# Linear attention and a gated convolution layer: queries projected with the tokens moving, their maxima subtracted by a third matmul pass

## The chip, the cores and the metric

One NeuronCore of a Trainium2 chip runs the whole program. The metric is the device time of one execution in microseconds (us), the median of several runs. TensorE (PE) multiplies matrices and writes PSUM; VectorE (DVE), ScalarE (ACT) and GpSimd (POOL) work on elements; SyncE (SP) here only issues DMA transfers, one after the other in a fixed order. Each engine works through its own instructions in order and waits on semaphores for the others.

## The reference

```python
def phi(x):                                   # x: batch 8, heads 8, 576 tokens, 64
    proj = np.einsum('bhsd,df->bhsf', x, w_phi)        # 64 -> 128 features
    proj = proj - np.max(np.abs(proj), axis=-1, keepdims=True)
    return np.concatenate([np.exp(proj), np.exp(-proj)], axis=-1)
q_p, k_p = (phi(q), phi(k))
kv = np.einsum('bhsf,bhsd->bhfd', k_p, v)
z = np.sum(k_p, axis=2)
num = np.einsum('bhsf,bhfd->bhsd', q_p, kv)
den = np.einsum('bhsf,bhf->bhs', q_p, z)[..., None] + 1e-06
attn = num / den                              # then 8 heads side by side: 512 columns
h = np.maximum(x @ w_in, 0.0)                 # 512 -> 1024
# conv_out: three-tap convolution over the tokens, per column
gate = 1.0 / (1.0 + np.exp(-conv_out))
out = h * gate @ w_out                        # 1024 -> 512
```

All inputs and outputs are float32. What matters here is that each token's query projection has the largest absolute value among its 128 features subtracted before the two exponentials.

## The kernel before, in words

**Units and groups.** The attention of a batch is two units (`qd` 0 and 1), each of four heads laid out as two pairs: a query tile has the 64 dimensions of two heads on its 128 partitions and tokens along its columns. A unit is cut into five groups: group 0 has one tile of 128 tokens (the last 64 tokens of both pairs), groups 1 to 4 have two tiles, so a unit has 9 tiles and the 16 units have 144. `k_process` does one group of keys, `q_process` one group of queries.

**Precision.** A float32 operand is cut by `split` into a rounded part `hi` (type fp32r, which TensorE multiplies in one pass) and the rest `lo = x - hi`. A product is then three fp32r passes: hi*hi, hi*lo and lo*hi. An operand that is left as float32 takes two passes, each at half the speed. The first `NQ_F32` = 2 units project their queries in float32.

**A group of queries before.** `load_split` loads a tile `qr` (line 179) and POOL makes `qxh` and `qxl` of it (lines 62 and 65). `project` (lines 199 to 201) multiplies with the tokens as the stationary operand and the block-diagonal weights `wbd` (256 columns: 128 features for each of the two heads) as the moving one, so the result `qp` has tokens on partitions. DVE takes the largest absolute value along the row (`qm`, line 204) and subtracts it (`qs`, line 206). TensorE then turns each 128x128 block (line 320, `tp`), since the next product needs features on partitions. ACT takes both exponentials from PSUM (line 326), `split` makes `qh` and `ql` (ACT line 60, DVE line 65), and the `nm` products (lines 348 and 356) give numerator and denominator. Small transfers carry denominators (line 377, `den`, and line 397, `rr`) to where one operation can divide.

**PSUM.** Pool `pg` has four banks under the tag `g`, shared by key projections, query projections, turned tiles and `nm`. Pool `pm` has two banks for the layer behind the attention, `pk` two for the key-value sums.

**The layer behind.** `h_part` (`hp`, line 429) and `o_part` (`op`, line 488) are long rows of fp32r passes, 24 of them for each of 64 output tiles in `o_part` and 12 for each of 128 in `h_part`; `conv_process` does the convolution and the gate on POOL, DVE and ACT (lines 452 to 475).

**The order.** The program text is not the order of work. A planner at the end of the kernel steps generators: each yields what it costs TensorE (`pe`), how long its inputs take (`wait`, times `LAT` = 1.7), and which named events it needs (`until`). It mixes attention and the layer behind by the work left in each (`ATT_PE`, `MOE_PE`), and up to `WINDOW` attention chains are under way. The order in which instructions are made sets their priority; a scheduler then places each on its engine by priority, as soon as its inputs are ready in the scheduler's own reckoning. `tc.high_priority()` puts instructions ahead of others. The resulting order on each engine is fixed before the kernel runs.

Of the kernel before, what the change touches and what calls it, by code (L numbers as in the profile page):

```python
# [16 lines left out]
F = 128  # L17
DM, FF = 512, 1024
P = 128
# [3 lines left out]
VW = D + 1  # L23
NH = 11

WINDOW = 13
LAT = 1.7
TAIL_US = 24
AHEAD = 300

NQ_F32 = 2
NKV_F32 = 2


# [1 line left out]
def kernel(  # L36
# [41 lines left out]
    split(wbd_f, wbd_hi, wbd_lo, nc.vector, nc.vector)  # L78
    idn = load_const(ident, [P, P], "idn")


    rr = cp.tile([P, S], F32, name="rr")
    nc.gpsimd.memset(rr, 0.0)

# [87 lines left out]
    def load_split(src, b, qd, g, kind):  # L172
        c0, n = group_columns(g)
        if kind == "q" and 2 * b + qd < NQ_F32:
            raw = sb.tile([P, n * P], F32, name=f"{kind}r{b}_{qd}_{g}", tag=kind + "xh", bufs=2)
            nc.sync.dma_start(out=raw, in_=src[b, qd, :, c0 : c0 + n * P])
            return n, raw, None
        raw = sb.tile([P, n * P], F32, name=f"{kind}r{b}_{qd}_{g}", tag=kind + "r", bufs=2)
        nc.sync.dma_start(out=raw, in_=src[b, qd, :, c0 : c0 + n * P])
        hi = sb.tile([P, n * P], F32R, name=f"{kind}xh{b}_{qd}_{g}", tag=kind + "xh", bufs=2)  # L180
        lo = sb.tile([P, n * P], F32R, name=f"{kind}xl{b}_{qd}_{g}", tag=kind + "xl", bufs=2)
        split(raw, hi, lo, nc.gpsimd, nc.gpsimd)
        return n, hi, lo

    def project(n, hi, lo, b, qd, g, kind):

        if b == 0 and kind == "k":

            ps = pm.tile([P, n * 256], F32, name=f"{kind}p{b}_{qd}_{g}", tag="m")
        else:  # L190
            ps = pg.tile([P, n * 256], F32, name=f"{kind}p{b}_{qd}_{g}", tag="g", bufs=4)
        for t in range(n):
            o = ps[:, t * 256 : (t + 1) * 256]
            his = hi[:, t * P : (t + 1) * P]
            if lo is None:
                nc.tensor.matmul(out=o, lhsT=his, rhs=wbd_f, start=True, stop=True)
                continue
            los = lo[:, t * P : (t + 1) * P]
            nc.tensor.matmul(out=o, lhsT=his, rhs=wbd_hi, start=True, stop=False)  # L199
            nc.tensor.matmul(out=o, lhsT=his, rhs=wbd_lo, start=False, stop=False)  # L200
            nc.tensor.matmul(out=o, lhsT=los, rhs=wbd_hi, start=False, stop=True)  # L201
        ps3 = ps.rearrange("p (t f) -> p t f", f=F)
        m = sb.tile([P, 2 * n], F32, name=f"{kind}m{b}_{qd}_{g}", tag="m", bufs=4)
        nc.vector.tensor_reduce(out=m, in_=ps3, axis=AX, op=ALU.max, apply_absolute_value=True)  # L204
        pr = sb.tile([P, 2 * n, F], F32, name=f"{kind}s{b}_{qd}_{g}", tag=kind + "s", bufs=2)
        nc.vector.tensor_tensor(out=pr, in0=ps3, in1=m.unsqueeze(2).broadcast_to([P, 2 * n, F]), op=ALU.subtract)  # L206
        return pr

# [11 lines left out]
    def k_process(b, qd, g):  # L220
        j = (b * NQ + qd) * 5 + g

        def back(key, k):
            return (key, j - k) if j >= k else None

        yield until(back("kp", 2), back("kv", 4))
        n, hi, lo = load_split(kT, b, qd, g, "k")
        v0 = 16 if g == 0 else 4 * (g - 1)
        v = sb.tile([P, 4 * VW], F32, name=f"v{b}_{qd}_{g}", tag="v", bufs=4)
        nc.sync.dma_start(out=v, in_=vt[b, qd, :, v0 * VW : (v0 + 4) * VW])  # L230
        yield wait(3000)
        yield until(back("kv", 2))
        set_ready(("kp", j))
        pr = project(n, hi, lo, b, qd, g, "k")
        e = sb.tile([P, 2, 2 * n, F], F32, name=f"ke{b}_{qd}_{g}", tag="ke", bufs=2)
        nc.scalar.activation(out=e[:, 0], in_=pr, func=AF.Exp)  # L236
        nc.scalar.activation(out=e[:, 1], in_=pr, func=AF.Exp, scale=-1.0)
        yield pe(330 * n)
        yield wait(3000)
        yield until(back("kv", 1))  # L240
        if g == 0:
            kvps[b, qd] = [pk.tile([P, 2, 2 * VW], F32, name=f"kv{b}_{qd}_{i}", tag=f"kv{i}") for i in range(2)]
        kp = kvps[b, qd]

        def products():
            for t in range(n):
                for i in range(2):
                    for s in range(2):
                        lhsT = e[:, s, 2 * t + i, :]
                        if g == 0:  # L250
                            ins = nc.tensor.matmul(out=kp[i][:, s, :], lhsT=lhsT, rhs=v[:, 2 * i * VW : 2 * (i + 1) * VW],  # L251
                                             start=(s == 0), stop=False, skip_group_check=True)
                        else:
# [46 lines left out]
    def q_process(b, qd, g):  # L300
# [7 lines left out]
        yield wait(3000)  # L308
        yield until(back("tp", 2))
        set_ready(("qp", *divmod(j, 5)))  # L310
        pr = project(n, hi, lo, b, qd, g, "q")
        yield pe(330 * n)
        yield wait(1700)
        yield until(back("num", 2))
        set_ready(("tp", *divmod(j, 5)))

        tp = pg.tile([P, 2, n, P], F32, name=f"tp{b}_{qd}_{g}", tag="g", bufs=4)
        for t in range(n):
            for i in range(2):
                nc.tensor.transpose(out=tp[:, i, t, :], in_=pr[:, 2 * t + i, :], identity=idn)  # L320
# [3 lines left out]
        for s in range(2):  # L324
            e = qh[:, s] if f32 else sb.tile([P, 2, n * P], F32, name=f"qe{b}_{qd}_{g}_{s}", tag="qe", bufs=2)
            nc.scalar.activation(out=e, in_=tp.rearrange("p i t s -> p i (t s)"), func=AF.Exp, scale=1.0 - 2.0 * s)  # L326
            if not f32:
                split(e, qh[:, s], ql[:, s], nc.scalar, nc.vector)
        yield pe(220 * n)
# [37 lines left out]
        for pr_, o, s0, w in parts:  # L367
            if (b, qd, pr_) not in den:
                den[b, qd, pr_] = sb.tile([72, 16], F32, name=f"den{b}_{qd}_{pr_}", tag="den", bufs=3)
                numt[b, qd, pr_] = sb.tile([P, S], F32, name=f"num{b}_{qd}_{pr_}", tag="num", bufs=4)  # L370
            dn, nt = den[b, qd, pr_], numt[b, qd, pr_]

            dro = dr[D : D + 1, 2 * o : 2 * (o + w)]
# [149 lines left out]
        active.append([now[0], g, False, lead[0]])  # L523

    MOE_PE = 2 * B * (8 * 1480 + 4 * 2960)
    ATT_PE = B * (18 * 330 + 72 * 215 + 18 * 550 + 8 * 6 * 270 + 4 * 250)
    TAIL = TAIL_US * 1000
    left = {"a": ATT_PE, "m": MOE_PE}
    start = {}
# [113 lines left out]
```

## Time and profile before

| | |
|---|---|
| Median of 3 runs | 825.25 us (824.22 to 826.01) |
| The profiled execution | 825.6 us, span 823.5 us, mean granted TensorE clock 0.989 |
| PE, share of the span busy | 96% |
| PE weight loads (overlap with PE) | 94% |
| DVE | 78% |
| ACT | 69% |
| POOL | 37% |
| DMA queue of SP, share of 16 engines | 20.1% |

The span runs from the first to the last instruction; the 2.1 us between it and the execution's time lie around it. A busy share says how much of the span an engine had an instruction under way. Matmuls overlap one another in the profile: one takes some 0.28 us from start to end, but the next starts much sooner, so the cost of a pass is the distance between the starts of two neighbours, not its duration.

### The profile page before, as it was taken

The page shows a single profiled execution, that of the slowest core. Times are in us where ns is not written, and L with a number is a line of the kernel's source. Part 1 is how long each engine was busy: PE and PEld are TensorE (multiplying, and loading weights), DVE is VectorE, ACT ScalarE, POOL GpSimd, SP SyncE. Part 2 cuts the span into 40 slices and gives each one's busy share as a digit, 9 for nine tenths or more (in the row PEclk, how much of TensorE's full clock was granted, in tenths as well). Part 3 has the DMA queues.
Part 4 walks back from the last instruction along what each step waited for, and adds up shares of the span by engine and source line. Part 5 has one row for each costly group of instructions (what it writes and reads, how often), then busy time and mean ns, then how long its engine had stood idle before and what let it go on. Part 6 is the DMA issues. An engine that isn't in the chain of part 4 may idle for free.

```text
span 823.5 us, 17817 instructions
## 1 busy us (share of the span) xinstructions
PE 788.0 (96%) x6350; PEld 772.5 (94%) x6350; DVE 645.6 (78%) x1390; ACT 569.5 (69%) x1228; POOL 307.6 (37%) x467
## 2 busy tenths in 40 slices
PE   7778779999999999999999999999999999999998
PEld 6767678999999999999999999999999999999998
DVE  4879999799987769787779878788697878766551
ACT  4598777797788867687586857678576867644332
POOL 4757765444443424414233333424334131111110
PEclk9799989999999999999999999999999999999999
DMA  6544421211211302121121211112021100000001
GB/s 187 157 134 135 135 66 47 67 41 44 70 56 44 93 18 71 27 82 50 46 61 43 69 34 60 47 50 82 15 77 29 56 12 19 13 30 30 23 23 44
DMA packets 56328, 49.18 MB, mean 60 GB/s; under 512 B 15024, under 2 KB 54192, under 8 KB 56240
## 3 DMA queue, kind: packets, MB, share of 16 engines
q1 hardware_dynamic: 56240, 48.05, 20.1%
q8 instruction: 51, 0.84, 0.4%
q14 instruction: 37, 0.30, 0.1%
HBM read 38.13 MB, written 9.44 MB: 58 GB/s over the span
## 4 chain that ended last, share of the span: by engine, by line
PE 74%; DVE 10%; ACT 7%; issue 4%; DMA 3%; POOL 1%; SPq 1%; DVEq 0%; ACTq 0%; POOLq 0%
PE op L488 22%; PE hp L429 21%; PE kv L255 8%; PE nm L356 8%; PE tp L320 3%; PE kp L199 2%; PE nm L348 2%; PE kp L200 2%; PE kp L201 2%; PE qp L199 1%; PE qp L200 1%; PE qp L201 1%; DMA w_r<-in_w_in_dram 1%; PE kv L251 1%; DVE qm L204 1%
## 5 line engine op out<-in xcount | busy, mean ns | idle before, releaser
L457 DVE SCALAR_TENSOR_TENSOR c<-h,cw,c 128x287 f32<-128x287 f32 (+1 forms) x256 | 138.7, 554 | 49.4 <-POOL c L452 47.5
L452 POOL TENSOR_SCALAR c<-h,cw 128x288 f32<-128x288 f32 x128 | 75.0, 588 | 243.6 <-ACT h L436 184.3
L255 PE MATMUL kv<-v,ke 128*128 128x65 f32 x1024 | 159.4, 255 | 1.4 <-ACT ke L236 1.2
L255 PEld LDWEIGHTS kv<-v,ke 128*128 128x128 f32 x1024 | 153.5, 193 | 4.8 <-ACT ke L236 1.8
L429 PE MATMUL hp<-xh,win_hi 128*128 128x290 f32 x512 | 153.2, 300 | 0.6 <-ACT os L493 0.6
L429 PE MATMUL hp<-xl,win_hi 128*128 128x290 f32 x512 | 152.7, 298 | 0.2 <-DVE xl L65 0.2
L488 PE MATMUL op<-gh,wout_hi 128*128 128x288 f32 x512 | 152.2, 298 | 0.0
L429 PE MATMUL hp<-xh,win_lo 128*128 128x290 f32 x512 | 151.9, 297 | 0.0
L488 PE MATMUL op<-gl,wout_hi 128*128 128x288 f32 x512 | 151.4, 296 | 0.0
L488 PE MATMUL op<-gh,wout_lo 128*128 128x288 f32 x512 | 150.9, 295 | 0.0
L436 ACT ACTIVATE h<-hp 128x290 f32<-128x290 f32 x128 | 52.2, 414 | 71.7 <-PE hp L429 71.2
L429 PEld LDWEIGHTS hp<-xh,win_hi 128*128 128x128 f32 x512 | 96.7, 190 | 1.5 <-ACT os L493 1.4
L62 POOL TENSOR_SCALAR kxh<-kr 128x256 fp32r<-128x256 f32 (+1 forms) x80 | 43.8, 547 | 144.1 <-PE kp L200 134.6
L429 PEld LDWEIGHTS hp<-xl,win_hi 128*128 128x128 f32 x512 | 97.0, 189 | 0.6 <-DVE xl L65 0.6
L429 PEld LDWEIGHTS hp<-xh,win_lo 128*128 128x128 f32 x512 | 97.1, 190 | 0.0
L488 PEld LDWEIGHTS op<-gh,wout_lo 128*128 128x128 f32 x512 | 96.4, 188 | 0.0
L488 PEld LDWEIGHTS op<-gl,wout_hi 128*128 128x128 f32 x512 | 96.2, 188 | 0.0
L488 PEld LDWEIGHTS op<-gh,wout_hi 128*128 128x128 f32 x512 | 96.1, 188 | 0.0
L65 DVE TENSOR_TENSOR ql<-qe,qh 128x512 fp32r<-128x512 f32 x112 | 79.9, 732 | 9.9 <-ACT qh L60 9.5
L236 ACT ACTIVATE ke<-ks 128x512 f32<-128x512 f32 (+1 forms) x80 | 46.9, 586 | 39.1 <-DVE ks L206 36.5
L326 ACT ACTIVATE qe<-tp 128x512 f32<-128x512 f32 x112 | 61.2, 595 | 12.2 <-PE tp L320 10.4
L356 PE MATMUL nm<-ql,kvh 128*65 128x256 f32 x224 | 68.4, 308 | 0.3 <-DVE ql L65 0.2
(84 smaller groups left out, 1989.5 us busy)
## 6 DMA issues: line engine op xcount, KB each, us to landing
v<-in_vt_dram SPq DMA_DIRECT2D x80, 130.0 KB
out_dram<-os SPq DMA_DIRECT2D x64, 144.0 KB
qr<-in_qT_dram SPq DMA_DIRECT2D x64, 128.0 KB
kr<-in_kT_dram SPq DMA_DIRECT2D x64, 128.0 KB
w_r<-in_w_in_dram SPq DMA_DIRECT2D x8, 512.0 KB
w_r<-in_w_out_dram SPq DMA_DIRECT2D x8, 512.0 KB
rr<-rc SPq DMA_DIRECT2D x128, 2.2 KB
qr<-in_qT_dram SPq DMA_DIRECT2D x16, 64.0 KB
```

Source lines behind the costliest of these rows:

```text
L62: nc.gpsimd.tensor_scalar(out=hi, in0=src, scalar1=1.0, scalar2=0.0, op0=ALU.mult, op1=ALU.add)
L65: eng_lo.tensor_tensor(out=lo, in0=src, in1=hi.bitcast(F32), op=ALU.subtract)
L199: nc.tensor.matmul(out=o, lhsT=his, rhs=wbd_hi, start=True, stop=False)
L236: nc.scalar.activation(out=e[:, 0], in_=pr, func=AF.Exp)
L255: ins = nc.tensor.matmul(out=kp[i][:, s, p0 : p0 + VW], lhsT=lhsT, rhs=v[:, (2 * t + i) * VW : (2 * t + i + 1) * VW], start=False, stop=(g ...
L326: nc.scalar.activation(out=e, in_=tp.rearrange("p i t s -> p i (t s)"), func=AF.Exp, scale=1.0 - 2.0 * s)
L356: ins = after(ins, lambda: nc.tensor.matmul(out=ps[:, i, o : o + w], lhsT=w_, rhs=x_, start=(k == 0), stop=(k == 5)))
L429: nc.tensor.matmul(out=ps, lhsT=w_, rhs=x_, start=(k == 0), stop=(k == 11))
L436: nc.scalar.activation(out=hs, in_=ps, func=AF.Relu)
L452: nc.gpsimd.tensor_scalar(out=cv, in0=hs[:, o : o + TC], scalar1=cw[:, f, 1:2], scalar2=0.0, op0=ALU.mult, op1=ALU.add)
L457: nc.vector.scalar_tensor_tensor(out=cv[:, lo:hi], in0=hs[:, o + j - 1 + lo : o + j - 1 + hi], scalar=cw[:, f, j : j + 1], in1=cv[:, lo:hi ...
L488: nc.tensor.matmul(out=ps, lhsT=w_, rhs=x_, start=(k == 0), stop=(k == 23))
```

## The change

From unit 4 on (`NQ_F32` = 4, so from the third batch) a group of queries goes another way; units 2 and 3 move from three fp32r passes to float32.

The input tile `qx` now has 128 partitions for one head at a time: rows 0 to 63 hold the rounded query, rows 64 to 127 the rest; the two heads and the tiles of the group lie side by side in up to 512 columns. To that end the query is loaded twice (two DMAs), ACT rounds all 128 rows and POOL subtracts on the lower 64. The weights are stationary: `wq_hi` holds the rounded weights in both halves, `wq_lo` the rest of the weights over rows 0 to 63 and zeros below. Two passes of up to 512 columns give the whole projection with features on partitions, so nothing has to be turned. The maximum now runs across partitions: DVE takes it inside blocks of 32 features with a transposing reduction (`qmt`, 16 columns of 128 rows), three ACT copies bring the four blocks of partitions together, three small DVE operations form the maximum as a rounded part and a rest (in `mx`), a DVE transpose lays them out as rows (`qmp`), and two DMAs write them over rows 64 and 65 of `qx`. A third pass with `wq_m`, which is -1 in those two rows and 0 elsewhere, adds minus the maximum to the PSUM bank. Both exponentials then read this bank as before.

Buffers: `WINDOW` 13 to 16; `qs` 3 instead of 2 for queries, `v` and `num` 3 instead of 4. The planner's costs for TensorE follow.

```diff
-WINDOW = 13
+WINDOW = 16
-NQ_F32 = 2
+NQ_F32 = 4
...
+    for i in range(2):
+        r = slice(D * i, D * i + D)
+        nc.gpsimd.tensor_copy(out=wq_hi[r, :], in_=wbd_hi[r, i * F : (i + 1) * F].bitcast(F32))
+    nc.gpsimd.tensor_copy(out=wq_m, in_=rr[:, 0:F])
+    nc.gpsimd.tensor_copy(out=wq_lo, in_=rr[:, 0:F])
+    nc.gpsimd.tensor_copy(out=wq_lo[0:D, :], in_=wbd_lo[0:D, 0:F].bitcast(F32))
+    nc.gpsimd.tensor_scalar(out=wq_m[D : D + 2, :], in0=rr[D : D + 2, 0:F], scalar1=-1.0, scalar2=0.0, op0=ALU.add, op1=ALU.add)
+    mx = [cp.tile([32, 32], F32, name=f"mx{i}") for i in range(2)]
...
+        if kind == "q":
+            raw = sb.tile([P, 2, n * P], F32, name=f"qr{b}_{qd}_{g}", tag="qr", bufs=2)
+            for h in range(2):
+                nc.sync.dma_start(out=raw[D * h : D * h + D, :, :],
+                                  in_=src[b, qd, :, c0 : c0 + n * P].rearrange("(i d) s -> d i s", d=D))
+            x = sb.tile([P, 2, n * P], F32R, name=f"qx{b}_{qd}_{g}", tag="qs", bufs=3)
+            nc.scalar.activation(out=x, in_=raw, func=AF.Copy)
+            nc.gpsimd.tensor_tensor(out=x[D:P], in0=raw[D:P], in1=x[D:P].bitcast(F32), op=ALU.subtract)
+            return n, x, x
...
+            x = hi
+            tp = pg.tile([P, 2, n, P], F32, name=f"qp{b}_{qd}_{g}", tag="g", bufs=4)
+            tpf, xf = tp.rearrange("p i t s -> p (i t s)"), x.rearrange("p i s -> p (i s)")
+            c = w // 32
+            nc.tensor.matmul(out=tpf, lhsT=wq_hi, rhs=xf, start=True, stop=False, skip_group_check=True)
+            nc.tensor.matmul(out=tpf, lhsT=wq_lo, rhs=xf, start=False, stop=False, skip_group_check=True)
+
+            mt = sb.tile([P, 4, 16], F32, name=f"qmt{b}_{qd}_{g}", tag="qmt", bufs=2)
+            with tc.high_priority():
+                nc.vector.tensor_reduce(out=mt[:, 0, 0:c], in_=tpf.rearrange("p (c f) -> p c f", f=32), axis=AX,
+                                        op=ALU.max, apply_absolute_value=True, apply_transpose=True)
+                for a in range(1, 4):
+                    nc.scalar.activation(out=mt[0:32, a, 0:c], in_=mt[32 * a : 32 * a + 32, 0, 0:c], func=AF.Copy)
+                m = sb.tile([32, 32], F32, name=f"qm{b}_{qd}_{g}", tag="qm", bufs=2)
+                mp = mx[j % 2]
+                mr = mt[0:32, :, 0:c].rearrange("p a c -> p c a")
+                nc.vector.tensor_reduce(out=mp[:, 0:c].bitcast(F32R), in_=mr, axis=AX, op=ALU.max)
+                nc.vector.tensor_reduce(out=m[:, 0:c], in_=mr, axis=AX, op=ALU.max)
+                nc.vector.tensor_tensor(out=mp[:, 16 : 16 + c].bitcast(F32R), in0=m[:, 0:c], in1=mp[:, 0:c], op=ALU.subtract)
+                mpt = sb.tile([32, 32], F32, name=f"qmp{b}_{qd}_{g}", tag="qmp", bufs=2)
+                nc.vector.transpose(out=mpt, in_=mp)
+                for i in range(2):
+                    nc.sync.dma_start(out=xf[D + i : D + i + 1, :].bitcast(F32).rearrange("k (c t) -> k c t", t=32),
+                                      in_=mpt[16 * i : 16 * i + c, :])
+            yield pe(230 * n)
+            yield wait(4000)
+            yield until(back("num", 2))
+            set_ready(("tp", *divmod(j, 5)))
+            with tc.high_priority():
+                nc.tensor.matmul(out=tpf, lhsT=wq_m, rhs=xf, start=False, stop=True, skip_group_check=True)
+            yield pe(115 * n)
...
-            nc.scalar.activation(out=e, in_=tp.rearrange("p i t s -> p (i t s)"), func=AF.Exp, scale=1.0 - 2.0 * s)
+            with tc.high_priority():
+                nc.scalar.activation(out=e, in_=tps, func=AF.Exp, scale=1.0 - 2.0 * s)
```

More of the change, by code (lines that the diff above doesn't have):

```diff
@@ L79 @@
     idn = load_const(ident, [P, P], "idn")
+    wq_hi = cp.tile([P, F], F32R, name="wq_hi")
+    wq_lo = cp.tile([P, F], F32R, name="wq_lo")
+    wq_m = cp.tile([P, F], F32R, name="wq_m")
     rr = cp.tile([P, S], F32, name="rr")
     nc.gpsimd.memset(rr, 0.0)
+    for i in range(2):
[6 more added lines that the diff above has]
+    mx = [cp.tile([32, 32], F32, name=f"mx{i}") for i in range(2)]
+    for t in mx:
+        nc.gpsimd.memset(t, 0.0)
     bias_e = cp.tile([P, 1], F32, name="bias_e")
@@ L174, in load_split @@
         if kind == "q" and 2 * b + qd < NQ_F32:
-            raw = sb.tile([P, n * P], F32, name=f"{kind}r{b}_{qd}_{g}", tag=kind + "xh", bufs=2)
+            raw = sb.tile([P, n * P], F32, name=f"{kind}r{b}_{qd}_{g}", tag=kind + "r", bufs=2)
             nc.sync.dma_start(out=raw, in_=src[b, qd, :, c0 : c0 + n * P])
             return n, raw, None
+        if kind == "q":
[7 more added lines that the diff above has]
+            return n, x, x
         raw = sb.tile([P, n * P], F32, name=f"{kind}r{b}_{qd}_{g}", tag=kind + "r", bufs=2)
@@ L204, in project @@
         nc.vector.tensor_reduce(out=m, in_=ps3, axis=AX, op=ALU.max, apply_absolute_value=True)
-        pr = sb.tile([P, 2 * n, F], F32, name=f"{kind}s{b}_{qd}_{g}", tag=kind + "s", bufs=2)
+        pr = sb.tile([P, 2 * n, F], F32, name=f"{kind}s{b}_{qd}_{g}", tag=kind + "s", bufs=3 if kind == "q" else 2)
         nc.vector.tensor_tensor(out=pr, in0=ps3, in1=m.unsqueeze(2).broadcast_to([P, 2 * n, F]), op=ALU.subtract)
@@ L228, in k_process @@
         v0 = 16 if g == 0 else 4 * (g - 1)
-        v = sb.tile([P, 4 * VW], F32, name=f"v{b}_{qd}_{g}", tag="v", bufs=4)
+        v = sb.tile([P, 4 * VW], F32, name=f"v{b}_{qd}_{g}", tag="v", bufs=3)
         nc.sync.dma_start(out=v, in_=vt[b, qd, :, v0 * VW : (v0 + 4) * VW])
@@ L310, in q_process @@
         set_ready(("qp", *divmod(j, 5)))
[L311 to L320, printed above, removed]
+        w = n * 2 * P
+        if lo is None:
+            pr = project(n, hi, lo, b, qd, g, "q")
+            yield pe(330 * n)
+            yield wait(1700)
+            yield until(back("num", 2))
+            set_ready(("tp", *divmod(j, 5)))
+            tp = pg.tile([P, 2, n, P], F32, name=f"tp{b}_{qd}_{g}", tag="g", bufs=4)
+            for t in range(n):
+                for i in range(2):
+                    nc.tensor.transpose(out=tp[:, i, t, :], in_=pr[:, 2 * t + i, :], identity=idn)
+            yield pe(220 * n)
+        else:
+            x = hi
[18 more added lines that the diff above has]
+                nc.vector.transpose(out=mpt, in_=mp)
+                for i in range(2):
+                    nc.sync.dma_start(out=xf[D + i : D + i + 1, :].bitcast(F32).rearrange("k (c t) -> k c t", t=32),
+                                      in_=mpt[16 * i : 16 * i + c, :])
+            yield pe(230 * n)
+            yield wait(4000)
+            yield until(back("num", 2))
+            set_ready(("tp", *divmod(j, 5)))
+            with tc.high_priority():
+                nc.tensor.matmul(out=tpf, lhsT=wq_m, rhs=xf, start=False, stop=True, skip_group_check=True)
+            yield pe(115 * n)
@@ L324, in q_process @@
         for s in range(2):
+            tps = tp.rearrange("p i t s -> p i (t s)")
             e = qh[:, s] if f32 else sb.tile([P, 2, n * P], F32, name=f"qe{b}_{qd}_{g}_{s}", tag="qe", bufs=2)
-            nc.scalar.activation(out=e, in_=tp.rearrange("p i t s -> p i (t s)"), func=AF.Exp, scale=1.0 - 2.0 * s)
+            with tc.high_priority():
+                nc.scalar.activation(out=e, in_=tps, func=AF.Exp, scale=1.0 - 2.0 * s)
             if not f32:
                 split(e, qh[:, s], ql[:, s], nc.scalar, nc.vector)
-        yield pe(220 * n)
         yield wait(3000)
@@ L369, in q_process @@
                 den[b, qd, pr_] = sb.tile([72, 16], F32, name=f"den{b}_{qd}_{pr_}", tag="den", bufs=3)
-                numt[b, qd, pr_] = sb.tile([P, S], F32, name=f"num{b}_{qd}_{pr_}", tag="num", bufs=4)
+                numt[b, qd, pr_] = sb.tile([P, S], F32, name=f"num{b}_{qd}_{pr_}", tag="num", bufs=3)
             dn, nt = den[b, qd, pr_], numt[b, qd, pr_]
@@ L525 @@
     MOE_PE = 2 * B * (8 * 1480 + 4 * 2960)
-    ATT_PE = B * (18 * 330 + 72 * 215 + 18 * 550 + 8 * 6 * 270 + 4 * 250)
+    ATT_PE = B * (18 * 330 + 72 * 215 + 18 * 345 + 8 * 6 * 270 + 4 * 250) + NQ_F32 // NQ * 18 * 205
     TAIL = TAIL_US * 1000
```

## The prediction

> **What bounds the kernel now.** I read the busy shares first, then the busy time by stage, then the waits, and only then single instructions.
>
> ```profile
> PE 788.0 (96%) x6350; PEld 772.5 (94%) x6350; DVE 645.6 (78%) x1390; ACT 569.5 (69%) x1228; POOL 307.6 (37%) x467
> ...
> 0.00:190.00 190.00, 159.04 (x1198) 147.21 (x1199) 162.71 (x315) 142.43 (x306) 116.07 (x148) 0.96 0.36 106
> 190.00:700.00 510.00, 509.65 (x4270) 507.52 (x4269) 413.33 (x910) 374.22 (x808) 175.33 (x288) 1.00 0.18 50
> ...
> 327.00:423.00 96.00, 95.94 (x804) 95.52 (x804) 77.28 (x170) 69.11 (x150) 33.73 (x57) 1.00 0.19 53
> 423.00:519.00 96.00, 95.94 (x804) 95.40 (x802) 76.86 (x169) 69.31 (x150) 33.98 (x57) 1.00 0.19 53
> 519.00:615.00 96.00, 95.95 (x804) 95.50 (x803) 76.85 (x169) 69.20 (x150) 33.77 (x57) 1.00 0.19 53
> ```
>
> The window rows give, after the length, busy time and count for PE, PEld, DVE, ACT and POOL, then the granted clock. Up to 190 us PE is idle for a sixth of the time: other work sets the pace there. From 190 to 700 us PE is busy for 509.65 of 510 us at full clock. The last three rows are one batch each: the kernel has become periodic, 96 us a batch, and repeats itself to within 0.01 us of PE time. So a microsecond of PE work taken out of a batch there shortens the batch by a microsecond, unless PE begins to wait. It does not wait now. DVE is busy for 77 us of the 96, ACT for 69.
>
> A busy PE says nothing on what a pass costs, since passes overlap. I take the distance between starts:
>
> ```profile
> 419.91 0.28 PE L199 MATMUL qp<-wbd_hi,qxh 128*128 128x256 f32 x1
> 420.03 0.28 PE L200 MATMUL qp<-wbd_lo,qxh 128*128 128x256 f32 x1
> 420.15 0.28 PE L201 MATMUL qp<-wbd_hi,qxl 128*128 128x256 f32 x1
> 420.26 0.29 PE L429 MATMUL hp<-xl,win_hi 128*128 128x290 f32 x1
> ...
> 178.20 3.21 PE hp L429 x24
> ...
> 61.41 0.49 PE L320 MATMUL tp<-idn,qs 128*128 128x128 f32 x3
> ...
> L320 PE MATMUL tp<-idn,qs x288: 270/272/448, 13.7 to 700.4; 128*128 128x128 f32 x144
> ...
> 58.92 0.60 PE L348 MATMUL nm<-qh,kvh 128*65 128x256 f32 x2
> L348 PE MATMUL nm<-qh,kvh 128*65 128x256 f32 x64 | 19.5, 386 | 1.6 <-ACT qh L326 1.6
> ```
>
> The first four rows are of the timeline: three 256-column fp32r passes start 0.35 us apart in all, so 0.118 each. Twenty-four 290-column passes take 3.21 us on the chain (0.134 each). Three turns end 0.49 us after the first starts, and one lasts 0.272, so they are 0.109 apart. Two float32 passes of 256 columns last 0.60, one 0.386: 0.214 apart.
>
> **The change part by part: PE.** A group of two tiles costs 6 x 0.118 + 4 x 0.109 = 1.144 us now. Afterwards it is three fp32r passes of 512 columns, a size the trace does not have. From one side, scaling 0.134 from 290 columns to 512 gives 0.237; from the other, the float32 pass streams its 256 columns at half speed, which is as many steps, in 0.214. One has the type, the other the length; I take the middle, 0.226, and keep both ends. That is 0.678, a saving of 0.466. A group of one tile goes from 3 x 0.118 + 2 x 0.109 = 0.572 to 0.354, a saving of 0.218. A batch has eight of the first and two of the second: 4.16 us. Six batches: 25.0 (23.3 to 26.7).
>
> [...]
>
> Units 2 and 3 go from three fp32r passes a tile (0.354) to two float32 ones (0.428): 18 x 0.074 = 1.3 us more, in the stage where PE has idle time, so 1.3 is the upper end and I count it.
>
> ```profile
> L199 PE MATMUL qp<-wbd_hi,qxh x126: 276/283/383, 76.1 to 692.8; 128*128 128x256 f32 x126
> ```
>
> These 126 tiles run from 76 to 693 us, 4.9 us a tile; the third batch starts 18 tiles in, at about 164 us. So a quarter of its saving falls before 190 us, where PE isn't the limit: 1.1 us that does not count.
>
> **Other engines.** What they lose and gain, from these rows:
>
> ```profile
> L204 DVE TENSOR_REDUCE qm<-qp 128x4 f32<-128x512 f32 x64 | 43.0, 678 | 0.8 <-PE qp L201 0.8
> L206 DVE TENSOR_TENSOR qs<-qp,qm 128x512 f32<-128x512 f32 x64 | 43.0, 678 | 0.1
> L392 DVE TENSOR_SCALAR den<-den 72x16 f32<-72x16 f32 x32 | 8.3, 260 | 15.4 <-DMA den<-dr 9.8 <-issue 5.6
> L60 ACT ACTIVATE qh<-qe 128x512 fp32r<-128x512 f32 x112 | 65.7, 635 | 0.1
> L379 ACT ACTIVATE num<-nm 64x64 f32<-64x64 f32 x64 | 13.8, 216 | 1.1
> L62 POOL TENSOR_SCALAR qxh<-qr 128x256 fp32r<-128x256 f32 x56 | 26.4, 473 | 62.3 <-PE qp L200 62.1
> L65 POOL TENSOR_TENSOR qxl<-qr,qxh 128x256 fp32r<-128x256 f32 x56 | 47.4, 854 | 1.7
> L65 POOL TENSOR_TENSOR wout_lo<-w_t,wout_hi 128x512 fp32r<-128x512 f32 x8 | 11.2, 1399 | 3.1 <-ACT wout_hi L60 3.1
> ```
>
> DVE loses a reduction and a subtraction of 512 columns a group (1.36 us). It gains one reduction of as many columns through a 32x32 transpose, which no row shows: 0.68 if the turn costs nothing, 1.36 if it doubles it; I take 0.68, the row with the same operation and size. It also gains four small operations, 0.26 each by the 16-column row at most. Net about +0.4 us a two-tile group, 4 us a batch: 81 of 92. ACT gains the rounding (0.64) and three copies of 16 columns (0.22 each, by the 64-column row): 1.3 us a group, 13 a batch: 82 of 92. POOL loses 1.33 and gains about 1.4: nothing. Neither DVE nor ACT becomes the bound, so I cost their work at nothing; the cover is the 10 us that each has left in a batch of 92. If it were gone, the first to suffer would be `hp`, whose two banks are emptied by ACT.
>
> The preparation of `wq_hi`, `wq_lo` and `wq_m` on POOL is six small operations in the first microseconds, when PE waits for DMA: nothing, up to 2 us. The second load of a query and the finer rows double some 7 MB; the queue's transfers fill 20% of 16 engines: nothing, for they are fetched a group ahead. The buffers that shrink (`v`, `num`) and `WINDOW` alter the order in ways I can't price: 0, within 2 us either way.
>
> **The new wait.** Between the second and the third pass stand the reduction, three ACT copies, four DVE operations, two DMA issues and a landing.
>
> ```profile
> L397 SPq DMA_DIRECT2D rr<-rc x128: 704/728/1091, 52.9 to 725.8; - x128
> L377 SPq DMA_DIRECT2D den<-dr x96: 502/582/1059, 39.8 to 709.0; - x96
> ...
> 119.89 1.72 DMA den<-dr
> 254.59 1.83 DMA rr<-rc
> ...
> L392 DVE TENSOR_SCALAR den<-den x24: 156/171/399, 199.5 to 710.7; 72x16 f32<-72x16 f32 x24
>   DMA den<-dr: 7.2, 9
> ...
> L405 DVE STREAM_SHUFFLE xf<-rr x50: 473/482/506, 196.5 to 743.6; 128x290 f32<-128x290 f32 x50
>   DMA rr<-rc: 15.6, 7
> ```
>
> That is 0.68 + 0.65 + 1.0 + 2 x 0.6 + 1.8 = 5.3 us with nothing in the way; the planner sets 6.8 us aside, which PE fills with the layer behind. What counts is whether the chain on the chip is later than in the order's own reckoning: then PE, which is in order, stands still, and all of `hp`, `op`, `nm` and `kv` queued behind the third pass with it. The third pass is put ahead of others, so it gets little room. The trace has two hops of this kind, both small DMAs whose reader is ahead of others on DVE. From 190 us on, `den` made DVE wait 7.2 us over 24 uses (0.30 each), `rr` 15.6 us over 25 (50 shuffles, two a transfer): 0.62. For PE, the same order left 0.35 us of idle time in 510 us. So the wait lies between 0 and 0.62 us a group. I take half of the `den` value, 0.15: it is the nearer in number of issues (each of these waits for the last of two or three, `rr` for four), halved because PE runs behind everything else, as its full busy time shows. Sixty groups: 9 us. The same SP queue carries 60 more loads and 120 short moves, some 110 us of issuing at 0.4 to 0.7 each; a load or an `out` store that waits at its head delays the move behind it. That is in the range, not in the sum.
>
> **The sum.** 825.6 (the profiled execution) - 25.0 + 1.3 + 1.1 + 9.0 = 812.0. The median shown is 0.35 below the profiled execution, so 811.6; I say 811.
>
> **The rivals.**
>
> *The chain is fully hidden.* For it: PE waits for nothing now, and the planner's 6.8 us exceed the 5.3. Against it: the two DMA hops that do wait. Time: 825.25 - 25.0 + 1.3 + 1.1 = 803; with passes of 0.214 it is 801.
>
> *The waits eat the gain.* At (25.0 - 1.3 - 1.1) / 60 = 0.38 us a group PE's waits equal its saving. Between 0.35 and 0.40 the time is 824 to 827. For it: the `den` hop at 0.30 is not far. Against it: this needs just that value.
>
> *Slower: the third pass waits as `rr` does.* Place: PE in front of the `wq_m` pass, for the two moves on SP. Price: 0.62 us x 60 = 37, so 803 + 37 = 840. It decides from 0.38 us a group on. For it: two issues one behind the other and other issues between them, on a queue with a third more to do; the three ACT copies sit in order behind whatever ACT is doing. Against it: the `rr` readers wait in 7 of 25 cases only, and DVE has no backlog to hide in.
>
> *ACT becomes the limit.* 82 of 92 us leaves 10, and a batch would have to find more than 92 of ACT work. If ACT's waits push the batch back by 2 us the time is 803 + 12 = 815, inside my range.
>
> **Chances.** The forecast (gain in part, 804 to 823.5): 0.56. Fully hidden (below 804): 0.17. Eaten (within 0.2%, 823.6 to 826.9): 0.07. Slower: 0.20. About 0.2% is what a measurement of this kernel tells from no change. Faster is thus 0.73, same 0.07, slower 0.20. For eight in ten the range reaches from 799 (hidden, the short pass, 2 us from the order) to 834, which leaves out the upper half of the slower case. The likeliest case's own range is 804 to 823.
>
> **What the changed profile would show.** PE's instructions `tp` (line 320) are gone after the second batch, and the passes on `wq` stand 0.21 to 0.24 us apart. A batch in the middle takes 92 to 94 us. The idle time of PE ahead of the `wq_m` pass, released by the move's DMA, sums to about 9 us; near zero speaks for the first rival, above 23 for the slower one. The transposing reduction takes about 0.68 us, ACT is busy for some 640 us in all, DVE for about 670. I am wrong if the 512-column pass costs far more than 0.237, if the reduction takes over 2 us, or if PE waits at `hp` for ACT.

## The result, and the profile after

The changed kernel takes 847.24 us (median; 846.93 to 850.16) against 824.8 for the kernel before in the same comparison: a ratio of 1.028, interval 1.025 to 1.030. It is slower by 22 us. The forecast was 811, faster, with a range up to 834.

The page of the changed kernel, its busy shares:

```profile
PE 784.7 (93%) x5972; PEld 746.8 (88%) x5972; DVE 654.0 (77%) x1570; ACT 637.9 (75%) x1468; POOL 313.8 (37%) x395
```

The windows of the changed kernel (length, then busy time and count of PE, PEld, DVE, ACT and POOL, granted clock, DMA share, GB/s):

```profile
0.00:190.00 190.00, 160.55 (x1138) 145.14 (x1138) 161.95 (x330) 142.68 (x314) 104.13 (x126) 0.95 0.36 106
190.00:700.00 510.00, 482.81 (x3776) 461.51 (x3777) 404.79 (x1030) 423.88 (x1000) 187.90 (x232) 0.99 0.23 64
```

PE has 378 fewer instructions, but between 190 and 700 us it is now idle for 27.2 us of 510, where it was idle for 0.35. ACT is busy for 424 us of these 510 instead of 374; DVE and POOL hardly differ. The first 190 us are as before. So the loss lies in the stretch where PE had been full.

The passes of the new way, from PE's timeline:

```profile
435.28 0.39 PE L354 MATMUL qp<-qx,wq_lo 128*128 128x512 f32 x1
435.51 0.28 PE L416 MATMUL nm<-qh,kvl 128*65 128x256 f32 x1
```

A 512-column pass holds PE for 0.23 us (the median distance to the next start is 0.235). With 0.235 a batch saves 8 x (1.144 - 0.705) + 2 x 0.218 = 3.95 us, and six batches 23.7. The saving is there; it was not turned into time.

Whom PE waits for, 190 to 700 us (total, times, longest, in us):

```profile
PE nm L416 <- ACT num L439: 4.4, 5, 2.1
PE qp L378 <- DMA qx<-qmp: 3.3, 5, 1.7
PE kv L279 <- ACT ke L260: 2.5, 2, 1.6
PE qp L353 <- POOL qx L200: 2.5, 3, 1.2
PE qp L353 <- issue: 2.4, 2, 1.6
PE qp L353 <- DVE ks L230: 1.9, 4, 0.8
PE kp L223 <- ACT num L439: 1.8, 1, 1.8
```

The third pass (L378) has 3.3 us of it. Over the whole list, of which these are the longest rows, 14.4 us end with ACT, 3.7 with DVE, 3.0 with POOL, and 2.9 with nothing that the profile shows ("issue"). So about half of the idle time ends when ACT has emptied a PSUM bank or made an input. `hp` and `op`, for whose banks PE waits too, have 1.8 us together.

Behind some of these waits ACT itself had been standing, in front of an instruction that the change put on it. PE stands from 389.5 to 391.6 us for `num`; shortly before, ACT stood for 2.16 us at a rounding whose load had not landed:

```profile
388.30 0.63 ACT L199 ACTIVATE qx<-qr 128x512 fp32r<-128x512 f32 x1 [2.16 <-DMA qr<-in_qT_dram]
```

The waits of this kind are 4.3 us in front of the rounding (for the load) and 9.6 us in front of the copies of the maxima (for DVE's reduction), from 190 to 700 us:

```profile
ACT qmt L361 <- DVE qmt L358: 9.6, 7, 4.8
ACT qx L199 <- DMA qr<-in_qT_dram: 4.3, 3, 2.2
```

### The profile page after: what moved, and what is told of

It is laid out like the page before. It is cut to its first block, busy times and chain, and to the rows that moved or that the text cites. A ratio compares the mean times of both kernels' runs of the same rounds, so it can differ in the third digit from the quotient of the medians.

```text
span 845.1 us, 17785 instructions
## 1 busy us (share of the span) xinstructions
PE 784.7 (93%) x5972; PEld 746.8 (88%) x5972; DVE 654.0 (77%) x1570; ACT 637.9 (75%) x1468; POOL 313.8 (37%) x395
## 4 chain that ended last, share of the span: by engine, by line
PE 54%; ACT 18%; DVE 13%; DMA 7%; issue 5%; SPq 2%; POOL 2%; ACTq 0%; DVEq 0%; POOLq 0%
PE op L548 16%; PE hp L489 16%; PE kv L279 7%; PE nm L416 6%; DVE c L517 3%; PE nm L408 2%; ACT qh L60 2%; ACT qe L387 2%; ACT num L439 2%; DVE ql L65 2%; ACT qx L199 1%; DMA qr<-in_qT_dram 1%; DMA w_r<-in_w_in_dram 1%; ACT c L521 1%; PE qp L220 1%
## 5 line engine op out<-in xcount | busy, mean ns | idle before, releaser
L512 POOL TENSOR_SCALAR c<-h,cw 128x288 f32<-128x288 f32 x128 | 87.4, 686 | 229.5 <-ACT h L496 192.9
L489 PE MATMUL hp<-xh,win_hi 128*128 128x290 f32 x512 | 155.9, 306 | 3.6 <-ACT os L553 1.4
L489 PE MATMUL hp<-xl,win_hi 128*128 128x290 f32 x512 | 155.1, 303 | 0.0
L489 PE MATMUL hp<-xh,win_lo 128*128 128x290 f32 x512 | 154.3, 301 | 0.0
L200 POOL TENSOR_TENSOR qx<-qr,qx 64x512 fp32r<-64x512 f32 (+1 forms) x60 | 77.6, 1296 | 137.6 <-ACT qx L199 99.0
L65 DVE TENSOR_TENSOR ql<-qe,qh 128x512 fp32r<-128x512 f32 x112 | 92.3, 838 | 28.3 <-ACT qh L60 28.0
L489 PEld LDWEIGHTS hp<-xl,win_hi 128*128 128x128 f32 x512 | 99.3, 194 | 1.2 <-DVE den L452 0.2
L489 PEld LDWEIGHTS hp<-xh,win_lo 128*128 128x128 f32 x512 | 99.1, 194 | 0.4
L62 POOL TENSOR_SCALAR kxh<-kr 128x256 fp32r<-128x256 f32 (+1 forms) x80 | 41.3, 518 | 103.1 <-PE kp L224 72.1
L416 PE MATMUL nm<-qh,kvh 128*65 128x256 f32 x224 | 62.6, 287 | 7.0 <-ACT num L439 4.4
```

The source lines that it names most:

```text
L62: nc.gpsimd.tensor_scalar(out=hi, in0=src, scalar1=1.0, scalar2=0.0, op0=ALU.mult, op1=ALU.add)
L65: eng_lo.tensor_tensor(out=lo, in0=src, in1=hi.bitcast(F32), op=ALU.subtract)
L200: nc.gpsimd.tensor_tensor(out=x[D:P], in0=raw[D:P], in1=x[D:P].bitcast(F32), op=ALU.subtract)
L416: ins = after(ins, lambda: nc.tensor.matmul(out=ps[:, i, o : o + w], lhsT=w_, rhs=x_, start=(k == 0), stop=(k == 5)))
L489: nc.tensor.matmul(out=ps, lhsT=w_, rhs=x_, start=(k == 0), stop=(k == 11))
L512: nc.gpsimd.tensor_scalar(out=cv, in0=hs[:, o : o + TC], scalar1=cw[:, f, 1:2], scalar2=0.0, op0=ALU.mult, op1=ALU.add)
```

## The experiments

The theories. **A**: the chain between second and third pass holds a PSUM bank of tag `g` for long, and its next tenant waits. **B**, later **E**: ACT has too much to do and comes late. **C**: the moves land late and PE stands in front of the third pass. **D**: the sizes that changed alongside cost the time. **O**: the order of the kernel before was a good one, and any other order loses.

All results; idle time of PE is the length of the window 190 to 700 us less PE's busy time in it:

| run | us | ratio to before (interval) | PE idle, us |
|---|---|---|---|
| before | 825.6 | | 0.4 |
| changed | 847.2 | 1.028 (1.025 to 1.030) | 27.2 |
| e1_sizes | 841.6 | 1.018 (1.015 to 1.021) | 5.4 |
| e2_no_chain | 839.5 | 1.017 (1.014 to 1.019) | 22.9 |
| e3_aside | 864.9 | 1.048 (1.045 to 1.050) | 33.5 |
| e4_dve_copies | 869.5 | 1.053 (1.050 to 1.055) | 41.4 |
| p1_window16 | 829.5 | 1.004 (1.003 to 1.006) | 4.6 |
| p2_f32_4 | 827.5 | 1.002 (1.001 to 1.003) | 1.5 |
| p3_bufs3 | 829.3 | 1.004 (1.003 to 1.006) | 3.3 |
| p4_window12 | 840.2 | 1.016 (1.013 to 1.019) | 6.7 |
| r3_sizes_back | 855.6 | 1.038 (1.034 to 1.042) | 30.5 |
| r4_nochain_sizes | 835.8 | 1.013 (1.011 to 1.014) | 18.4 |
| e5_pool_round | 852.3 | 1.032 (1.028 to 1.035) | 29.7 |
| r7_evict_first | 849.4 | 1.030 (1.024 to 1.035) | 27.2 |
| x1_nochain_pool | 831.3 | 1.007 (1.005 to 1.010) | 18.0 |
| x3_act_more | 857.1 | 1.038 (1.035 to 1.041) | 17.5 |
| x4_pool_all | 855.1 | 1.034 (1.030 to 1.038) | 33.9 |
| p5_lat | 831.2 | 1.006 (1.004 to 1.009) | 5.2 |
| x6_act_small | 844.4 | 1.023 (1.021 to 1.025) | 14.7 |
| x7_bank3 | 845.5 | 1.024 (1.021 to 1.027) | 8.1 |

The kernel before was run again beside each group: 825.4 to 826.1. Two expectations start from other figures for PE's idle time, 48 us in the changed kernel (r7) and 31 us without the chain (x1); what this table counts is 27.2 and 22.9, so their thresholds can't be read against it as they stand.

**The sizes alone** (e1_sizes, on the kernel before):

```diff
-WINDOW = 13
+WINDOW = 16
-NQ_F32 = 2
+NQ_F32 = 4
...
-        v = sb.tile([P, 4 * VW], F32, name=f"v{b}_{qd}_{g}", tag="v", bufs=4)
+        v = sb.tile([P, 4 * VW], F32, name=f"v{b}_{qd}_{g}", tag="v", bufs=3)
...
-                numt[b, qd, pr_] = sb.tile([P, S], F32, name=f"num{b}_{qd}_{pr_}", tag="num", bufs=4)
+                numt[b, qd, pr_] = sb.tile([P, S], F32, name=f"num{b}_{qd}_{pr_}", tag="num", bufs=3)
```

> The kernel before with the sizes alone of the change: WINDOW 16, NQ_F32 4, v and num with 3 buffers; the way of the queries is the old one. Theory A (the chain between second and third pass holds a PSUM bank of tag g for 18 us, and PE waits for the next bank): no part of the loss is here, 825 to 828 us, 1.3 us of it for the float32 projection of units 2 and 3. Theory B (ACT has too much to do and is late): the same. Theory C (the moves land late and PE stands in front of the third pass): the same. Theory D (the smaller buffers and the wider window cost what is lost): 840 us or more.

16 us slower, in D's range: theory D, which I had priced at nothing, has a part. A and C cannot touch this kernel. Only 5 us of it is idle time of PE after 190 us; the first 190 us do less PE work as well:

```profile
0.00:190.00 190.00, 155.47 (x1122) 142.84 (x1123) 162.08 (x317) 138.22 (x297) 96.81 (x123) 0.93 0.35 104
190.00:700.00 510.00, 504.56 (x4248) 502.27 (x4248) 410.24 (x889) 371.10 (x798) 176.84 (x292) 1.00 0.18 50
```

**No chain** (e2_no_chain, on the changed kernel):

```diff
-            mt = sb.tile([P, 4, 16], F32, name=f"qmt{b}_{qd}_{g}", tag="qmt", bufs=2)
-            with tc.high_priority():
...
-                    nc.sync.dma_start(out=xf[D + i : D + i + 1, :].bitcast(F32).rearrange("k (c t) -> k c t", t=32),
-                                      in_=mpt[16 * i : 16 * i + c, :])
```

> The changed kernel without the chain: reduction, ACT copies, small DVE operations and the two moves are left out, the third pass follows with nothing to wait for, so the maximum isn't subtracted from the queries of units 4 to 15. Theories A and C: the whole PE saving shows, 802 to 808 us, and PE is busy for over 99% from 190 to 700 us. Theory B: ACT still rounds (35 us) but does not copy (38 us less), so about half of the loss stays: 815 to 825 us. Theory D: 825 us or more.

Without reduction, copies and moves, and with a third pass that waits for nothing, it is still 14 us slower than before. Of the four only D allowed for that. A and C fall as the whole explanation: PE idles for 23 us with no chain at all. The waits of PE in this run, 190 to 700 us:

```profile
PE op L531 <- ACT os L536: 8.7, 6, 1.8
PE qp L353 <- ACT qe L370: 7.8, 4, 2.2
```

Both are banks that ACT has to empty. At 514 us its timeline shows why one is late:

```profile
514.09 1.28 ACT L504 ACT_TABLE_LOAD   x1
515.38 2.13 ACT L504 ACTIVATE c<-c 128x2304 f32<-128x2304 f32 x1
517.53 0.41 ACT L536 ACTIVATE os<-op 128x288 f32<-128x288 f32 x1
```

A table load and the sigmoid of a whole token block, 3.4 us in one piece, stand in front of the `os` that frees an `op` bank. It is so each time: PE has nine waits of 1.5 us or more in this run, 16.7 of the 22.9 us, and in each of them ACT had started such a sigmoid 2.6 to 5.2 us before PE went on. The block is no part of the change. The kernel before has it too, with the table load at 442.96 us for instance, and PE doesn't wait there. So here it is not new work that PE waits for, but old work that now stands in front of what PE needs next.

**The chain aside** (e3_aside):

```diff
+                spare = sb.tile([2, 384], F32, name=f"qsp{b}_{qd}_{g}", tag="qsp", bufs=1)
-                    nc.sync.dma_start(out=xf[D + i : D + i + 1, :].bitcast(F32).rearrange("k (c t) -> k c t", t=32),
-                                      in_=mpt[16 * i : 16 * i + c, :])
+                    nc.sync.dma_start(out=spare[i : i + 1, 0 : 32 * min(c, 12)].rearrange("k (c t) -> k c t", t=32),
+                                      in_=mpt[16 * i : 16 * i + min(c, 12), :])
```

> The changed kernel with the whole chain at work, but its two moves write a spare tile (12 of the 16 pieces of each row) and the third pass waits for nothing, so the maximum isn't subtracted. All engines and SP have the load of the changed kernel; the bank is held only until reduction and exponentials are done. Theories A and C: 805 to 815 us. Theory B: ACT's load is unchanged, so 835 to 847 us. Theory D: 835 us or more.

865 us: with the wait taken away and the work left, it is 18 us slower than the changed kernel. A missed by 50 us and C with it, B by 18; D's "835 us or more" takes the result in, but has no upper end. The edit takes away a dependency, so the scheduler places instructions in another order, and that this order is the worse one is the likely reason; no run separates the two. PE's waits in it are again for ACT, `op` behind `os` above all (9.0 us).

**The copies on DVE** (e4_dve_copies):

```diff
-                    nc.scalar.activation(out=mt[0:32, a, 0:c], in_=mt[32 * a : 32 * a + 32, 0, 0:c], func=AF.Copy)
+                    nc.vector.tensor_copy(out=mt[0:32, a, 0:c], in_=mt[32 * a : 32 * a + 32, 0, 0:c])
```

> The changed kernel with the three copies of the maxima on DVE instead of ACT; the result is the same. Theory A: the chain loses a hop to ACT and back (some 2.5 us of 12.6), so a part comes back: 835 to 843 us. Theory B: 38 us less on ACT, 830 to 838 us. Theory C: the moves are as they were, 845 us or more.

869, the slowest of all. A and B missed; C's "845 us or more" takes it in, and PE's wait for the moves in front of the third pass did grow, from 3.3 to 10.0 us after 190 us, 7 of the 22 us lost. ACT has 39 us less to do (599 in all), DVE 43 more (697), and PE idles more. Less work on ACT bought nothing when it went to an engine that was as full.

**Single sizes, and an order of no meaning**, on the kernel before: WINDOW 16 (p1), NQ_F32 4 (p2), three buffers (p3), WINDOW 12 (p4), and LAT 1.6 (p5).

> The kernel before with WINDOW 16 alone. Theory D1 (the wider window lets more chains start, so attention work is queued in front of the evictions): most of the 16 us that the sizes together cost is here, 836 to 842 us. Theory D2 (float32 projection of units 2 and 3) and D3 (fewer buffers): 825 to 828 us. Theory O (the kernel before sits at a lucky order, and any change of the order costs some 10 to 20 us): 832 to 845 us, here and in the three beside it alike.

> The kernel before with NQ_F32 4 alone: units 2 and 3 are projected in float32. D2: 836 to 842 us. D1 and D3: 826 to 828, the 1.3 us that the passes cost. Theory O: 832 to 845 us.

> The kernel before with 3 buffers instead of 4 for v and num, alone. D3: 836 to 842 us, with loads of v that start later. D1 and D2: 825 to 827 us. Theory O: 832 to 845 us.

> The kernel before with WINDOW 12, a change that no kernel here makes: one chain fewer under way, no work added. Theory O: 832 to 845 us, with new idle time of PE after 190 us. D1, D2 and D3 say nothing of it; if the window were free, 824 to 828 us.

> The kernel before with LAT 1.6 instead of 1.7 in the planner, which alters the order of work and nothing else. Theory O: 832 to 845 us, like WINDOW 12. If the order matters little: 823 to 829 us.

No single size is the culprit: 3.8, 1.8 and 3.6 us, together 9 of e1's 16. But WINDOW 12 costs 14.5 us and LAT 1.6 costs 5.7, neither of which adds any work. Theory O is right in sign each time, but its range of 832 to 845 held for WINDOW 12 alone: the sizes are 2 to 15 us, not always 10 or more. That is what the order of this kernel is worth by itself.

**Sizes put back** (r3_sizes_back; r4_nochain_sizes also has four buffers for `v`):

```diff
-WINDOW = 16
+WINDOW = 13
-NQ_F32 = 4
+NQ_F32 = 2
```

> The changed kernel with WINDOW 13 and NQ_F32 2 as before (v and num stay at 3 buffers, SBUF has no room for more), so the new way begins with the second batch. Theory D (the sizes cost 16 us, as in the run with the sizes alone): 830 to 836 us. Theory E (ACT has more to do and comes late to the banks that PE needs next, whatever the sizes): 842 to 852 us. Theory O (each new order draws its own loss): anything from 825 to 865 us.

> The changed kernel without the chain (no maximum is subtracted from these queries), with WINDOW 13, NQ_F32 2 and v with 4 buffers as before. Theory D: 839 less 16, 820 to 825 us. Theory E: ACT still rounds, 832 to 840 us. If the new way of projecting costs PE what was reckoned and nothing waits: 800 to 805 us.

In the changed kernel the old sizes are worse by 8 us, though they also send the second batch the new way; without the chain they are better by 4. D's ranges missed both times, so a fixed price of 16 us for the sizes does not carry over to this kernel. E's 832 to 840 held for r4; r3 is 4 us above its range.

**Rounding on POOL, and banks emptied first** (e5_pool_round, r7_evict_first):

```diff
-            nc.scalar.activation(out=x, in_=raw, func=AF.Copy)
+            nc.gpsimd.tensor_scalar(out=x, in0=raw, scalar1=1.0, scalar2=0.0, op0=ALU.mult, op1=ALU.add)
```

```diff
-            nc.scalar.activation(out=hs, in_=ps, func=AF.Relu)
+            with tc.high_priority():
+                nc.scalar.activation(out=hs, in_=ps, func=AF.Relu)
```

(and the same for `os`.)

> The changed kernel with the rounding of the query on POOL instead of ACT: 35 us less on ACT, some 55 us more on POOL, the same result. Theory E: 830 to 840 us. Theory A (the chain holds the bank): 845 to 850 us. Theory O: anything from 835 to 865 us.

> The changed kernel with ACT's emptying of the hp and op banks (lines 496 and 553) put ahead of other work, nothing else altered. Theory E: PE's idle time after 190 us falls from 48 us by a third or more, 825 to 838 us. Theory A: these banks are not the ones that are short, 842 to 850 us. Theory O: anything from 825 to 865 us.

Neither helps: 852 and 849 (844.7 to 856.4). E as I had put it then misses both times; A's range holds for the second. With the banks of `hp` and `op` put first the idle time of PE stays at 27.2 us to the tenth. There was little to win: in the changed kernel PE waits 1.8 us for them.

**ACT's work by itself** (x3_act_more and x6_act_small, on the kernel before; x1_nochain_pool and x4_pool_all on the changed one):

```diff
+        if kind == "q" and 2 * b + qd >= 4:
+            pad = sb.tile([P, 256], F32, name=f"pad{b}_{qd}_{g}", tag="pad", bufs=1)
+            for _ in range(2 if n == 2 else 1):
+                nc.scalar.activation(out=pad[:, 0 : n * P], in_=raw, func=AF.Copy)
+            for _ in range(3):
+                nc.scalar.activation(out=pad[0:32, 0:16], in_=raw[0:32, 0:16], func=AF.Copy)
```

(x6_act_small has the second loop alone. x1_nochain_pool is e2_no_chain with the rounding on POOL; x4_pool_all is e5_pool_round with the three copies on POOL too.)

> The kernel before with useless copies on ACT for each group of queries from unit 4 on: two of 256 columns (one in a group of one tile) and three of 16 columns, some 79 us in all, where the changed kernel has 74; nobody reads them. PE's work is untouched. Theory E: PE begins to idle after 190 us, 838 to 855 us. Theory A (only the bank that the chain holds matters): 824 to 830 us. Theory O: 830 to 845 us, no more than WINDOW 12 alone.

> The kernel before with three useless ACT copies of 16 columns for each group of queries from unit 4 on, some 38 us of ACT work, nobody reads them. Theory E (PE loses 0.4 us for each us that ACT gets, as with 79 us): 836 to 844 us. If a copy costs by its place in the order and not by its length (three of five instructions): 843 to 850 us. Theory O: 829 to 840 us.

> The changed kernel without the chain (the maximum isn't subtracted from the queries of units 4 to 15), rounding on POOL: ACT has the work of the kernel before, PE the passes of the new way. Theory E (ACT's added work is what PE waits for): PE's idle time after 190 us falls from 31 to under 10 us, 805 to 818 us. Theory O (the new order loses by itself): 832 to 848 us.

> The changed kernel with rounding and the three copies of the maxima on POOL, the same result: ACT has the work of the kernel before, the chain and its moves stay. Theory E: 812 to 832 us. Theory A (the chain holds the bank, now longer): 845 to 860 us. Theory O: 835 to 865 us.

In x3 nobody reads the copies, PE's instructions are the same 6350, and ACT stays far below full (630 of 855 us). Yet 80 us of copies (60 us more of busy time, as neighbours overlap) cost 31 us, twice what WINDOW 12 cost. The short ones alone, 37.6 us, cost 18 (x6). E's ranges are passed by 2 and by 0.4 us, A's 824 to 830 is far off, and x6 lies in the 843 to 850 of a cost that goes by place and not by length. PE's waits in x3, 190 to 700 us:

```profile
PE nm L362 <- ACT qh L60: 7.1, 3, 2.5
PE kv L261 <- ACT ke L242: 4.5, 4, 1.8
PE op L494 <- ACT os L499: 2.0, 1, 2.0
```

But these copies add more than work. Each reads `qr`, so ACT, which goes in order, stands in front of them until that load has landed. The rows of x3 and then of x6, 190 to 700 us:

```profile
ACT pad L186 <- DMA qr<-in_qT_dram: 27.2, 14, 3.2
```

```profile
ACT pad L186 <- DMA qr<-in_qT_dram: 30.5, 20, 6.0
```

In the changed kernel this wait, in front of the rounding, is 4.3 us. And in x6 only 4.7 of PE's 14.7 us of idle time end with ACT; 6.3 end with DVE. So the two runs show that instructions on ACT's queue can cost 18 and 31 us while ACT is far from full. They give no price for a microsecond of ACT's work: work, a wait for a load and a new order came together.

The other direction, x1, takes ACT's added work out where there is no chain: 839.5 becomes 831.3. E's direction is right and its size is not (805 to 818 forecast): PE still idles for 18 us, 14.1 of them on ACT. The 8 us gained are no more than a change of order can do.

```profile
PE qp L353 <- ACT qe L370: 6.3, 4, 2.1
PE op L531 <- ACT os L536: 3.5, 4, 0.9
PE hp L472 <- ACT os L536: 2.8, 5, 1.1
```

The four waits for `qe` stand behind the sigmoid block again, as in e2.

x4 missed E's 812 to 832 by far: with ACT relieved and the chain kept it is 855, 24 us above x1. That lies in A's 845 to 860 (the chain holds the bank, now longer), and in O's range too.

One row of ACT goes along with these runs: how long it waits for `hp`, 190 to 700 us. Before:

```profile
ACT h L436 <- PE hp L429: 41.0, 32, 3.0
```

Changed:

```profile
ACT h L496 <- PE hp L489: 6.9, 10, 1.2
```

x3:

```profile
ACT h L442 <- PE hp L435: 21.2, 22, 2.8
```

x6:

```profile
ACT h L440 <- PE hp L433: 29.7, 25, 2.6
```

x1:

```profile
ACT h L479 <- PE hp L472: 20.3, 20, 1.9
```

Before, ACT stands ready for PE's next bank for 41 us of the 510: PE is the one that is late. In the changed kernel that is 7 us. A shorter PE work (x1) or a fuller ACT (x3, x6) each go with less of it, and each with idle time of PE. It is no measure of ACT's work alone: with one bank less and ACT's work as before (x7, below) it is 15.5 us. Nor does it rank the runs: x4 has 13.1 us of it and the second most idle time of PE.

**Three banks** (x7_bank3, on the kernel before):

```diff
-    pg = ctx.enter_context(tc.tile_pool(name="pg", bufs=4, space=bass.MemoryType.PSUM))
+    pg = ctx.enter_context(tc.tile_pool(name="pg", bufs=3, space=bass.MemoryType.PSUM))
```

> The kernel before with three g banks instead of four. The chain holds its bank for 17.9 us a group where the old way holds two in turn for 12.3 together, so at one group in some 10 us the changed kernel has 0.6 of a bank less to spare. Theory A (banks are short): a whole bank costs 40 us or more, 865 us and up. If banks are not short: 825 to 840 us, the latter by the order.

A whole bank less costs 19 us, half of what A asked for and a little more than the other case allowed (845.5 against 840). The changed kernel holds its bank for 17.9 us a group on average (first pass to the end of the second exponential), the old way two banks in turn for 12.3. At one group in 9.6 us that is 0.6 of a bank; by proportion some 11 us, an estimate from x7, or 5 if only the 8 us of idle time after 190 us count, where the changed kernel loses. e3, where the third pass has nothing to wait for, did not give these back, but its order is another one: the bank's part is neither shown nor excluded.

## Why the prediction was wrong

*PE is the bound from 190 us on.* The quoted windows were right, and the conclusion was only half right. "A microsecond of PE work taken out of a batch shortens the batch by a microsecond, unless PE begins to wait": it begins at once. x1 has the short PE work and no chain and no added ACT work, and it is 6 us slower than before. Between the starts of its passes the gaps (distances over 0.28 us, less 0.135) add up to 24 us more than before, and stretches of halved clock take 7 us more, most of them before 190 us: together more than what the passes save. In the changed kernel the gaps are 50 us more than before.

*The cost of a pass.* 0.226 was taken, 0.235 measured, the upper end being 0.237. Saving 23.7 instead of 25.0 us. Right. What the forecast calls half speed in float32 is, in the trace of before, 0.214 us for 256 columns against 0.118 in fp32r: 1.8 times as long.

*ACT costed at nothing.* This is the step that failed: the sum lets PE wait in front of the third pass alone, and costs the work of ACT and DVE at nothing. "The cover is the 10 us that each has left in a batch of 92" compares sums over a batch. After 190 us PE's waits that end with ACT add up to 14.4 us in the changed kernel and those that end with DVE to 3.7, against 3.3 in front of the third pass; before, all idle time there was 0.35. The sum of ACT's work was right (640 forecast, 637.9 measured). What it doesn't say is when each piece is done: ACT goes in order, so PE waits behind a block of 3.4 us (e2) or behind a rounding whose load has not landed (2.16 us of ACT, the changed kernel).

Why ACT comes late in the changed kernel is open in part. ACT can come late without its added work: x1 has none of it, and 14.1 us of PE's waits there end with ACT. Useless copies on ACT can bring it about in the old kernel, but they wait for a load besides (x3, x6). And giving ACT's added work to other engines did not help the changed kernel (e4, e5, x4). A row of before could have warned me: ACT waited for `hp` for 41 us of 510, PE being the late one, and I quoted busy shares instead. Nor did the first sign that I had named come: I had `hp` suffer first, and PE waits 1.3 us there; it waits at `nm`, `kv`, `kp` and the first pass of `qp`.

*The new wait.* The chain was reckoned at 5.3 us with nothing in the way; it takes 12.6 on average from the end of the second pass to the start of the third. The pieces are as forecast: reduction, copies, moves:

```profile
L358 DVE TRANSPOSE_TENSOR_REDUCE qmt<-qp x60: 401/702/719, 152.3 to 706.4; 128x16 f32<-128x512 f32 x48, 128x8 f32<-128x256 f32 x12
L361 ACT ACTIVATE qmt<-qmt x180: 206/213/217, 153.6 to 708.2; 32x16 f32<-32x16 f32 x144, 32x8 f32<-32x8 f32 x36
L371 SPq DMA_DIRECT2D qx<-qmp x120: 502/580/721, 158.2 to 714.3; - x120
```

The rest lies between the pieces. On average 1.7 us go by in front of the reduction, 1.8 in front of the copies, 0.8 in front of the first small DVE operation and 0.8 in front of the first issue; the four small DVE operations take 2.4 us from the first's start to the last's end, and 0.8 of it is their own time. What held each was not taken apart. And yet the price named for it was about right: 9 us forecast in front of the third pass, at most 7.6 measured in the whole span (PE and its weight loads together, two rows on what ended their idle time before line 378):

```profile
  DMA qx<-qmp: 5.7, 7
  issue: 1.9, 4
```

So the slower rival had the sign and nearly the time (840), by a mechanism that did not happen: it wanted 0.62 us a group in front of `wq_m` and there was at most 0.13. That its time came out near is luck. The rival "ACT becomes the limit" had the engine that half of the waits end with, and I left it at 2 us a batch because ACT would not be full. It isn't full; it is late.

*Sizes priced at 0, within 2 us.* Together 16 us on the kernel before, singly 2 to 4. The bound was too narrow. What they cost in the changed kernel is not the same: with WINDOW and NQ_F32 put back, that kernel was slower. So how much of the 22 us is theirs stays open.

**What stays open.** The steps from 825.6 (before) to 831.3 (x1: new passes, no chain, ACT as before) to 839.5 (e2: rounding on ACT) to 847.2 (changed: the chain) are measured, but they don't add up in another sequence: x4, with the chain and ACT relieved, is at 855. What the chain costs when its ACT part is elsewhere is 24 us (x4 against x1). The wait in front of the third pass is at most 14.1 us of it, and the bank is not excluded. Its DVE operations, put ahead of others, and the moves on SP, behind which `den` transfers are later (DVE waited 19.7 us for them from 190 to 700 us, 7.0 before), were not taken apart. No run tried the two exponentials without their new priority, or the planner's new costs by themselves. Against an order that was worth up to 15 us by itself (WINDOW 12), the steps of 6 to 8 us between these runs are no evidence of a cause.

## What to carry to other kernels

The sum of an engine's work over a batch doesn't say whether each piece comes in time. For every engine that feeds the busiest one, look for its longest blocks and for the instructions that will have to wait for something new; what stands behind them on that engine waits too, as `os` in e2 behind 3.4 us of table load and sigmoid. To see whether work on an engine "with room" can hurt, add useless work of that size to the kernel as it is and time it, but let it read something that has long been ready: the copies here waited for a load, and so do not give a price. Where an order is fixed ahead of time, change a constant that adds no work first, to learn how many microseconds the order is worth by itself.

## What was unexpected of the hardware

Three idle stretches of PE cost more than themselves here. In the changed kernel PE waits for ACT from 389.5 to 391.6 us; the windows there, with the granted clock as the sixth figure after the length (counts in brackets aside):

```profile
388.00:390.00 2.00, 1.47 (x10) 1.18 (x8) 1.02 (x2) 1.65 (x3) 0.94 (x1) 1.00 0.70 201
390.00:392.00 2.00, 0.44 (x2) 0.19 (x2) 1.77 (x3) 1.94 (x6) 0.33 (x1) 0.85 0.10 17
392.00:394.00 2.00, 2.00 (x9) 2.00 (x9) 1.52 (x4) 2.00 (x5) 0.51 (x1) 0.50 0.40 120
394.00:396.00 2.00, 2.00 (x18) 2.00 (x16) 1.32 (x5) 1.89 (x8) 0.51 (x1) 0.80 0.00 0
```

From the end of a wait of 2.1 us on, the granted clock is halved for about 3.4 us while PE is busy again: 9 matmuls in 2 us instead of the 18 two microseconds later. This happened three times between 190 and 700 us and took some 5 us in all; in the kernel before, never there. In all three cases PE had stood idle for 1.6 to 1.9 us of the 3.4 us ahead of it, not always in one piece. In x3 it happened five times. As much idle time did not always bring it: in the changed kernel PE waits for 1.83 us up to 242.5 us, and the granted clock is 1.00 from 240 to 246 us. What decides it was not shown.

The transposing reduction of 128x512 from PSUM takes 0.70 us, hardly more than the plain one of the kernel before (0.68): the 32x32 turn costs some 0.02 us here.
